# Convolution, routing and expert layers on one core: the first key's weights loaded and split one half batch earlier, the weights' transfers issued one step later and load first

## The chip, the cores and the metric

The kernel runs on one core of one Trainium2 chip. The metric is the device time of one execution in microseconds (us); lower is better. The engines are TensorE (PE, with its weight loads as PEld), VectorE (DVE), ScalarE (ACT), GpSimd (POOL) and SyncE (SP), which here only issues transfers.

## The reference

```python
# B = 8, S = 3584, D = 192; 8 heads of 24 channels, 7 taps
w = softmax(weight)                       # [8, 7]
out = einsum('hk,bskhg->bshg', w, unfold(pad(x)))   # causal convolution, per head
x = out.reshape(28672, 192)
logits = x @ w_gate                       # [28672, 8]
# greedy: all (token, expert) pairs in falling order of the logit; a token takes
# the first expert that has room; each expert takes 28672 / 8 = 3584 tokens
for e in range(8):
    h = maximum(x[mask_e] @ w1[e], 0)     # w1 192 x 1024
    out[mask_e] = h @ w2[e]               # w2 1024 x 192
```

## The kernel before

**Stage 1, convolution.** The tokens go through in 16 half batches of 1792. For each, `load` brings `X` in three transfers, `conv` makes eight PE products `cv` with a Toeplitz matrix (one per head), and ACT copies each into `a`; then ACT's queue issues the store `attn<-a`. The `cv` products take turns on four PSUM banks, so PE can be at most four ahead of ACT's copies. Between the heads, `mid(h)` puts in other work: DVE's transposes `aT<-a`, the gate products `pl` of an earlier half batch, their copy `L` on ACT, a transpose `pt`, and DVE's `M`. Pieces of the routing (who goes to which expert) are run by `bg.hook` as generators; their PE products and copies are named `bg`, `oa`, `X`, `asm`, `ja`. When the first list `ja` is there, GpSimd gathers (`xg`) the tokens of the first two tiles.

**Stage 2, expert layers.** `FFN.run` takes 56 tiles of 512 tokens. In a step `i` it runs, for `f` from 0 to 7: the first-layer product `ph` of tile `i` (`l1`, five matmuls), ACT's `hh` and DVE's `hl` from it, a part of the preparation of tile `i+1` (PE's `px`, then `xa` and `xd` on ACT and DVE), half of a second-layer product `y` of tile `i-1` (`l2`), and one call of `wsplit`. Matrices are kept as a high and a low float32r part, so that few passes give float32 accuracy.

**The weights.** A key is an expert at one of its visits. On the first visit, `wload` brings a part of the raw weights into a tile `raw` (pool `wr`, four buffers): `a` and `d` are halves of the first matrix (`d` in two transfers), `w` a quarter of the second. The pieces of a key come in the order a, d, a, d, w, w, w, w. `wsplit` takes the next piece, if its step has come: ACT copies the high part (`w<-raw`), an engine given by the caller subtracts for the low part (`w<-raw,w` or `dl<-raw,w`), SP stores both parts in DRAM (`kw`, `kd`, `kv`) for the second visit, and then the load of the piece four ahead is issued (lines 1200 to 1246). All these transfers stand in SP's one queue, in the order of the code, and each waits there for what it needs. Transfers also take eight completion semaphores in turn, and one waits for the transfer eight before it.

For the first key the four loads are issued at the start of half batch 13 (line 1554) and the first four pieces are split in half batches 14 and 15, at every other head, with GpSimd as the subtracting engine (line 1568). Its second matrix and all other keys are split by DVE in the steps of stage 2. Key 0's second matrix and key 1's first are split in step 0. After step 0, `tail` makes the gate products of half batches 14 and 15 on PE, each with `L`, a transpose and `M` behind it; then step 1 starts.

Of the kernel before, what the change touches and what calls it, by code (L numbers as in the profile page):

```python
# [6 lines left out]
F32 = mybir.dt.float32  # L7
# [21 lines left out]
class Meter:  # L29


    def __init__(self, pace, name, eng):
        self.pace, self.name, self.eng = pace, name, eng
# [1099 lines left out]
class FFN:  # L1133
# [3 lines left out]
    def __init__(self, tc, nc, attn, w1, w2, out, ident, wr, drm):  # L1137
        self.tc, self.nc = tc, nc

        self.kept1 = [drm.tile([128, 3, F], F32, name="kw%d" % e) for e in range(NE)]  # L1140
        self.keptd = [drm.tile([64, F], F32, name="kd%d" % e) for e in range(NE)]
        self.kept2 = [drm.tile([128, 8, 2 * D], F32, name="kv%d" % e) for e in range(NE)]
        self.attn, self.w1, self.w2, self.out, self.ident, self.wr = attn, w1, w2, out, ident, wr
        self.bg = lambda: None
        self.busy = lambda: False
        self.WT, self.RAW, self.XG, self.XT, self.H, self.Y, self.XS = {}, {}, {}, {}, {}, {}, {}
        self.wpa, self.wpb, self.DL = [None, None], [None, None], [None, None]
        self.scat, self.late = [], []
        self.free = set()
        self.xg = None  # L1150

# [47 lines left out]

    def wsplit(self, i, eng):  # L1200

        if self.done == len(self.pieces) or self.pieces[self.done][0] > i:
            return
        V, A = self.nc.vector, self.nc.scalar
        _, ky, j, what, q = self.pieces[self.done]
        wp = self.wpa[j]
        e = ky[0]
        if what == "W1" or (what, q) == ("a", 0):
            W = wp.tile([128, 3, F], FR, name="w1")
            self.WT[ky] = [W[:, 0], W[:, 1], W[:, 2], self.DL[j]]  # L1210
        if what == "W1":
            self.nc.sync.dma_start(W.bitcast(F32), self.kept1[e])
            self.nc.sync.dma_start(self.DL[j][0:64].bitcast(F32), self.keptd[e])
            self.done += 1
            return
        if what == "W2":
            t = self.wpb[j].tile([128, 8, 2 * D], FR, name="w2")
            self.WT[ky].append(t)
            self.nc.sync.dma_start(t.bitcast(F32), self.kept2[e])
            self.done += 1  # L1220
            return
        r = self.RAW.pop(self.done)
        if (what, q) == ("w", 0):
            self.WT[ky].append(self.wpb[j].tile([128, 8, 2 * D], FR, name="w2"))
        t = self.WT[ky]
        if what == "w":
            r = r[:, 0:2 * D].rearrange("p (k d) -> p k d", d=D)
            s = slice(2 * q, 2 * q + 2)
            hi, lo = t[4][:, s, 0:D], t[4][:, s, D:2 * D]
        else:  # L1230
            s = slice(512 * q, 512 * q + 512)
            hi, lo = (t[0][:, s], t[1][:, s]) if what == "a" else (t[2][:, s], t[3][0:64, s])
        A.activation(hi, r, AF.Copy)
        n = 64 if what == "d" else 128
        eng.tensor_tensor(lo, r[0:n], hi[0:n].bitcast(F32), op=OP.subtract)
        S = self.nc.sync
        if what == "w":
            S.dma_start(self.kept2[e][:, s], t[4][:, s].bitcast(F32))
        elif what == "a":
            S.dma_start(self.kept1[e][:, 0, s], hi.bitcast(F32))  # L1240
            S.dma_start(self.kept1[e][:, 1, s], lo.bitcast(F32))
        else:
            S.dma_start(self.kept1[e][:, 2, s], hi.bitcast(F32))
            S.dma_start(self.keptd[e][:, s], lo.bitcast(F32))
        self.done += 1
        self.wload()


    def gather(self, i, idx, rows=NTOK, clear=None):
# [162 lines left out]
def moe_kernel(ctx, tc, x, weight, wg, w1, w2, out):  # L1412
    nc = Pace(tc.nc)
    V, P = nc.vector, nc.gpsimd
# [4 lines left out]
    with ExitStack() as cw:  # L1419
# [11 lines left out]
        ff = FFN(tc, nc, attn, w1, w2, out, r.ident, wr, drm)  # L1431
# [99 lines left out]
        def hook(at):  # L1531
            nc.pe = max(nc.pe, PERIOD * at / 8 + START)
            bg.hook(1.5)
            if not got and len(bg.gens) == 4:
                first()
                got.append(at)
            elif got and at >= got[0] + 10 and at % 8 in (2, 5) and todo:
                for _ in range(2):
                    todo.pop(0)()
# [6 lines left out]
        for i in range(NHB):  # L1546
            if i + 3 < NHB:
                k.load(i + 3)
            if i == 4:
                r.consts_late()  # L1550
            if i == 13:
                cx[0].close()
                for _ in range(4):
                    ff.wload()
                ff.wpool(cw, 0, **late)

            def mid(h):

                if i and h == 0:
                    for u in range(4):  # L1560
                        left.append(partial(k.transp, i - 1, u))
                        if i > 1:
                            left.append(partial(gate, i - 2, u) if u < 3 else partial(end, i - 2))
                for _ in range(2 if got else 1):
                    if left and (i < LAG or got):
                        left.pop(0)()
                if i >= 14 and h % 2:
                    ff.wsplit(-1, P)
                hook(8 * i + h)

            k.conv(i, mid)
# [82 lines left out]
```

## Time and profile before

| | |
|---|---|
| three timed runs, us | median 1287.89, 1285.86 to 1289.23 |
| the profiled execution, us | 1280.46 |
| its span, first to last instruction, us | 1278.6 |
| mean granted clock of TensorE | 0.988 of 2.4 GHz |
| busy, us: PE, PEld | 1228.0 (96%), 1052.9 (82%) |
| busy, us: DVE, ACT, POOL | 993.4 (78%), 551.0 (43%), 510.0 (40%) |
| moved by DMA | 193.02 MB, 151 GB/s |

All rows are of the profiled execution. A time in a row counts from the start of the span. In a row of the windows, the first number after the stretch is its length; a busy time stands with the number of instructions in brackets. In a row of the timeline, `[1.80 <-ACT w L55]` means that the engine stood idle for 1.80 us before the instruction and that ACT's instruction on `w` ended that wait; `x4` means four such instructions, with their common length. A convolution product and a gate product are float32 and count as two matmuls each. SPq and ACTq are the issues of transfers. A line number of 55 is that of a helper that records every operation, so the names tell what an instruction is.

### The profile page before, as it was taken

The page shows a single profiled execution, that of the slowest core. Times are in us where ns is not written, and L with a number is a line of the kernel's source. Part 1 is how long each engine was busy: PE and PEld are TensorE (multiplying, and loading weights), DVE is VectorE, ACT ScalarE, POOL GpSimd, SP SyncE. Part 2 cuts the span into 40 slices and gives each one's busy share as a digit, 9 for nine tenths or more (in the row PEclk, how much of TensorE's full clock was granted, in tenths as well). Part 3 has the DMA queues.
Part 4 walks back from the last instruction along what each step waited for, and adds up shares of the span by engine and source line. Part 5 has one row for each costly group of instructions (what it writes and reads, how often), then busy time and mean ns, then how long its engine had stood idle before and what let it go on. Part 6 is the DMA issues. An engine that isn't in the chain of part 4 may idle for free.

```text
span 1278.6 us, 21798 instructions
## 1 busy us (share of the span) xinstructions
PE 1228.0 (96%) x7847; PEld 1052.9 (82%) x7847; DVE 993.4 (78%) x2229; ACT 551.0 (43%) x1220; POOL 510.0 (40%) x504
## 2 busy tenths in 40 slices
PE   5989979999999999999799999999999999999997
PEld 2445558889889888898689999999999999999997
DVE  7398569799989998998666777777777777777772
ACT  4544545856344434443243333333333333333332
POOL 3000335364354454343234444444444444444422
PEclk9999989999999999999899999999999999999999
DMA  9999797899533343433543423232413232231100
GB/s 239 345 332 301 249 330 262 277 316 320 187 105 133 102 151 95 148 131 104 126 131 101 165 76 102 96 117 74 151 47 113 77 102 97 68 120 47 47 25 29
DMA packets 100579, 193.02 MB, mean 151 GB/s; under 512 B 19232, under 2 KB 64752, under 8 KB 96240
## 3 DMA queue, kind: packets, MB, share of 16 engines
q1 hardware_dynamic: 57856, 115.15, 27.7%
q0 software_dynamic: 21504, 44.07, 11.6%
q10 hardware_dynamic: 21104, 32.34, 7.7%
q8 instruction: 63, 1.03, 0.3%
q14 instruction: 52, 0.43, 0.1%
HBM read 116.02 MB, written 75.50 MB: 150 GB/s over the span
## 4 chain that ended last, share of the span: by engine, by line
PE 85%; DMA 6%; DVE 5%; ACT 2%; issue 1%; POOL 1%; SPq 1%; POOLq 0%; ACTq 0%; DVEq 0%
PE ph L55 39%; PE y L55 38%; PE cv L55 3%; DMA X<-in_x_dram 3%; PE bg L55 3%; DMA raw<-in_moe_w_dram 2%; PE px L55 1%; DVE X L55 1%; PE pl L55 1%; DVE aT L55 1%; DVE hl L55 1%; ACT a_d L55 1%; POOL xg L1254 0%; DMA X<-otab 0%; ACT w L55 0%
## 5 line engine op out<-in xcount | busy, mean ns | idle before, releaser
L55 PE MATMUL y<-w,hh 128*128 128x384 f32 x1792 | 540.9, 357 | 0.0
L55 ACT ACTIVATE hh<-ph 128x512 fp32r<-128x512 f32 x448 | 268.1, 598 | 498.8 <-PE ph L55 497.6
L55 PE MATMUL y<-w,hl 128*128 128x192 f32 x1792 | 449.4, 251 | 0.0
L55 DVE SCALAR_TENSOR_TENSOR hl<-ph,hh 128x512 fp32r<-128x512 f32 x448 | 308.1, 688 | 146.2 <-ACT hh L55 142.2
L55 PE MATMUL ph<-xa,w 128*128 128x512 f32 x1344 | 396.4, 403 | 4.0 <-DVE hl L55 4.0
L55 PEld LDWEIGHTS y<-w,hl 128*128 128x128 f32 x1792 | 341.6, 191 | 15.1
L55 PEld LDWEIGHTS y<-w,hh 128*128 128x128 f32 x1792 | 337.0, 188 | 19.0 <-issue 2.2
L1329 POOL DMA_INDIRECT out_dram<-yo,ib x128 | 127.9, 999 | 288.4 <-DVE yo L55 278.6
L55 PEld LDWEIGHTS ph<-xa,w 128*128 128x128 f32 x1344 | 219.3, 190 | 24.8 <-DVE hl L55 5.6
L1329 POOL DMA_INDIRECT out_dram<-yo,ia x96 | 111.8, 1164 | 255.2 <-DVE yo L55 224.0
L55 DVE STREAM_TRANSPOSE xs<-xg 32x256 f32<-32x256 f32 x480 | 177.0, 369 | 8.2
L55 PE MATMUL ph<-xd,w 128*128 128x512 f32 x448 | 177.7, 397 | 1.7 <-DVE xd L55 1.7
L55 PE MATMUL ph<-xd,dl 128*128 128x512 f32 x448 | 174.9, 390 | 0.4 <-DVE dl L55 0.4
L1254 POOL DMA_INDIRECT xg<-attn,jb x128 | 138.2, 1080 | 57.1 <-issue 40.6
L1254 POOL DMA_INDIRECT xg<-attn,ja x96 | 110.3, 1149 | 32.1 <-issue 25.8
L55 PE MATMUL cv<-X,TH 118*128 118x384 f32 x256 | 102.8, 528 | 17.5 <-DVE TH L55 12.6
L55 ACT ACTIVATE yt<-y 128x192 f32<-128x192 f32 x224 | 73.6, 329 | 103.8 <-PE y L55 102.0
L55 DVE TENSOR_TENSOR yo<-y,yt 128x192 f32<-128x192 f32 x224 | 79.5, 355 | 40.3 <-ACT yt L55 37.6
L55 PEld LDWEIGHTS ph<-xd,w 128*128 128x128 f32 x448 | 84.3, 188 | 21.6 <-DVE xd L55 2.1
L55 PEld LDWEIGHTS ph<-xd,dl 128*128 128x128 f32 x448 | 84.5, 189 | 20.4 <-DVE dl L55 0.7
L55 PEld LDWEIGHTS cv<-X,TH 118*128 118x128 f32 x256 | 45.3, 197 | 51.5 <-issue 14.1
L55 ACT ACTIVATE a<-cv 128x384 f32<-128x384 f32 x128 | 59.6, 492 | 55.4 <-PE cv L55 37.7
(237 smaller groups left out, 901.3 us busy)
## 6 DMA issues: line engine op xcount, KB each, us to landing
w<-kw SPq DMA_DIRECT2D x16, 1536.0 KB, 8.0
w<-kv SPq DMA_DIRECT2D x16, 1536.0 KB, 7.1
attn<-a ACTq DMA_DIRECT2D x16, 1344.0 KB, 11.8
kw<-w SPq DMA_DIRECT2D x48, 256.0 KB, 4.3
kv<-w SPq DMA_DIRECT2D x32, 384.0 KB, 4.1
X<-in_x_dram SPq DMA_DIRECT2D x17, 672.0 KB, 14.5
X<-in_x_dram ACTq DMA_DIRECT2D x15, 672.0 KB, 10.9
raw<-in_moe_w_dram SPq DMA_DIRECT2D x32, 192.0 KB, 3.9
```

Source lines behind the costliest of these rows:

```text
L55: return f(*a, **k)
L1254: self.nc.gpsimd.indirect_dma_start(out=t[:, b], out_offset=None, in_=self.attn[0:rows], in_offset=bass.IndirectOffsetOnAxis(ap=idx[b], ax ...
L1329: st = self.nc.gpsimd.indirect_dma_start(out=self.out, out_offset=bass.IndirectOffsetOnAxis(ap=idx, axis=0), in_=o, in_offset=None, bounds ...
```

## The change

The four loads of the first key move from the start of half batch 13 to that of 12. The calls of `wsplit` in stage 1 begin in half batch 13 instead of 14, with DVE as the subtracting engine. And the transfers that belong to a piece (the load of a piece four ahead, and the stores) are kept as a function `moves`, which the next call of `wsplit` runs first; in it the load comes ahead of the stores.

```diff
     def wsplit(self, i, eng):
 
+        if self.moves:
+            self.moves()
+            self.moves = None
         if self.done == len(self.pieces) or self.pieces[self.done][0] > i:
             return
...
         S = self.nc.sync
-        if what == "w":
-            S.dma_start(self.kept2[e][:, s], t[4][:, s].bitcast(F32))
-        elif what == "a":
-            S.dma_start(self.kept1[e][:, 0, s], hi.bitcast(F32))
-            S.dma_start(self.kept1[e][:, 1, s], lo.bitcast(F32))
-        else:
-            S.dma_start(self.kept1[e][:, 2, s], hi.bitcast(F32))
-            S.dma_start(self.keptd[e][:, s], lo.bitcast(F32))
+
+        def moves():
+
+            self.wload()
+            if what == "w":
+                S.dma_start(self.kept2[e][:, s], t[4][:, s].bitcast(F32))
+            elif what == "a":
...
+        self.moves = moves
         self.done += 1
-        self.wload()
...
+            if i == 12:
+                for _ in range(4):
+                    ff.wload()
             if i == 13:
                 cx[0].close()
-                for _ in range(4):
-                    ff.wload()
                 ff.wpool(cw, 0, **late)
...
-                if i >= 14 and h % 2:
-                    ff.wsplit(-1, P)
+                if i >= 13 and h % 2:
+                    ff.wsplit(-1, V)
```

On ACT, this is the order around half batch 13 (`a<-cv` are the copies of the convolution, `w` the high parts of key 0, `X` and `asm` belong to the routing):

```order
 L204 DMA attn<-a 112x4x768
 L55 ACTIVATE a<-cv 128x16x24
+L55 ACTIVATE w_1442<-raw 128x512
 L55 ACTIVATE X_1119<-bg 128x512
 L55 ACTIVATE a<-cv 128x16x24 x2
-L55 ACTIVATE X_1465<-bg 128x1024 x2
+L55 ACTIVATE w_1442<-raw 128x512
+L55 ACTIVATE X_1474<-bg 128x1024 x2
+L55 ACTIVATE a<-cv 128x16x24 x2
+L55 ACTIVATE w_1442<-raw 128x512
+L55 ACTIVATE a<-cv 128x16x24
+L55 ACTIVATE asm<-bg 128x192
```

Three of the four copies now stand ahead of `asm`, and the fourth follows behind one more `a`; before, all four stood behind the next `attn`, in half batches 14 and 15.

On SP, this is the stretch of before behind the first loads of key 0 (`raw` of 128x2x192 is a quarter of the second matrix, `raw` of 128x512 or 64x512 belongs to the first matrix of key 1; `kw_83`, `kd_91` and `kv_99` are the stores of key 0):

```order
L1240 DMA kw_83<-w_1548 128x512
L1241 DMA kw_83<-w_1548 128x512
L1195 DMA raw<-in_moe_w_dram 128x2x192
L1243 DMA kw_83<-w_1548 128x512
L1244 DMA kd_91<-dl 64x512
L1195 DMA raw<-in_moe_w_dram 128x2x192
```

And this is the same stretch of the change:

```order
L1195 DMA raw<-in_moe_w_dram 128x2x192
L1247 DMA kw_83<-w_1442 128x512
L1248 DMA kw_83<-w_1442 128x512
L1195 DMA raw<-in_moe_w_dram 128x2x192
L1250 DMA kw_83<-w_1442 128x512
L1251 DMA kd_91<-dl 64x512
```

Each load now stands ahead of the two stores that it stood behind.

Later in SP's queue, around the fourth key (`kw_86`, `kd_94`), the routing writes a table and reads it back (`otab`, `X`). Before:

```order
L1240 DMA kw_86<-w_2650 128x512
L1241 DMA kw_86<-w_2650 128x512
L1195 DMA raw<-in_moe_w_dram 128x2x192
L542 DMA otab_82<-X_2311 128x2048
L559 DMA X_2711<-otab_81 16x16x128 x4
L559 DMA X_2711<-otab_82 16x16x128 x4
L1243 DMA kw_86<-w_2650 128x512
```

And with the change:

```order
L559 DMA X_2707<-otab_81 16x16x128 x4
L559 DMA X_2707<-otab_82 16x16x128 x4
L1195 DMA raw<-in_moe_w_dram 128x2x192
L1247 DMA kw_86<-w_2650 128x512
L1248 DMA kw_86<-w_2650 128x512
```

The first second-matrix load of that key moves from ahead of the table's transfers to behind them. Elsewhere PE, DVE and ACT keep their order in stage 2.

## Rows read from the trace of the kernel before

**Rows 1.** Windows: busy us of PE, PEld, DVE, ACT, POOL; clock; DMA share; GB/s:

```profile
160.00:180.00 20.00, 14.56 (x75) 9.93 (x77) 13.34 (x21) 9.69 (x20) 10.91 (x11) 0.89 0.95 303
...
180.00:200.00 20.00, 18.03 (x189) 15.18 (x182) 14.77 (x36) 9.27 (x23) 1.25 (x1) 0.94 0.88 308
...
280.00:300.00 20.00, 20.00 (x119) 18.13 (x118) 18.91 (x41) 14.79 (x40) 14.08 (x10) 1.00 0.97 324
```

**Rows 2.** Chain of waits, 159 to 183 us (start, length, what):

```profile
159.54 2.23 DMA kd<-dl
...
161.84 0.31 ACTq L204
...
165.86 8.89 DMA raw<-in_moe_w_dram
...
176.85 5.33 DMA raw<-in_moe_w_dram
...
182.20 0.63 ACT w L55
```

**Rows 3.** Timeline, ACT and DVE, 159 to 176 us (start, length, idle before):

```profile
159.98 1.29 ACT L55 ACTIVATE a<-cv 128x384 f32<-128x384 f32 x3
...
171.65 0.53 ACT L55 ACTIVATE w<-raw 128x384 fp32r<-128x384 f32 x1 [3.49 <-DMA raw<-in_moe_w_dram]
...
172.21 0.56 DVE L55 TENSOR_TENSOR w<-raw,w 128x384 fp32r<-128x384 f32 x1 [1.80 <-ACT w L55]
...
174.78 0.52 ACT L55 ACTIVATE w<-raw 128x384 fp32r<-128x384 f32 x1 [2.12 <-DMA raw<-in_moe_w_dram]
...
175.33 0.56 DVE L55 TENSOR_TENSOR w<-raw,w 128x384 fp32r<-128x384 f32 x1 [1.95 <-ACT w L55]
```

**Rows 4.** Timeline, SP's issues of the weights' transfers, 132 to 177 us:

```profile
132.01 0.47 SPq L1193 DMA_DIRECT2D raw<-in_moe_w_dram  x1
...
175.92 0.32 SPq L1238 DMA_DIRECT2D kv<-w  x1
...
176.28 0.52 SPq L1192 DMA_DIRECT2D raw<-in_moe_w_dram  x1
```

**Rows 5.** Instructions on the tile raw (ns min/median/max, first and last start):

```profile
L55 ACT ACTIVATE w<-raw x64: 508/578/641, 144.1 to 322.7; 128x512 fp32r<-128x512 f32 x32, 128x384 fp32r<-128x384 f32 x32
...
L55 DVE TENSOR_TENSOR w<-raw,w x46: 536/550/694, 167.6 to 324.7; 128x384 fp32r<-128x384 f32 x32, 128x512 fp32r<-128x512 f32 x14
...
L1235 POOL TENSOR_TENSOR w<-raw,w x2: 1280/1284/1288, 144.8 to 159.5; 128x512 fp32r<-128x512 f32 x2
...
DMA to landing us min/median/max: 2.8/4.3/9.5
```

**Rows 6.** Timeline, half batch 13: ACT, PE and DVE, 139 to 145 us:

```profile
139.03 1.94 ACT L55 ACTIVATE X<-bg 128x1024 bf16<-128x1024 bf16 x2 [0.53 <-PE bg L55]
...
141.80 2.83 PE L55 MATMUL cv<-X,TH 118*128 118x384 f32 x8
...
142.37 0.18 DVE L55 TENSOR_SCALAR m_f<-asm 128x32 f32<-128x32 f32 x1 [6.78 <-ACT asm L55]
```

**Rows 7.** Timeline, PE, the gate products of half batches 14 and 15:

```profile
179.00 2.79 PE L55 MATMUL bg<-aT,c_mu 128*32 128x128 f32 x48
...
183.46 1.52 PE L55 MATMUL bg<-aT,c_mu 128*32 128x128 f32 x48
```

**Rows 8.** Windows of 2 us around two falls of the granted clock:

```profile
174.00:176.00 2.00, 0.87 (x4) 0.37 (x2) 0.67 (x2) 1.01 (x2) 1.70 (x2) 0.87 1.09 315
...
182.00:184.00 2.00, 0.80 (x21) 0.68 (x25) 1.02 (x3) 1.23 (x4) 0.00 (x0) 0.92 1.04 353
...
622.00:624.00 2.00, 0.00 (x0) 0.00 (x0) 1.83 (x7) 0.00 (x0) 0.00 (x0) 0.66 1.15 95
```

**Rows 9.** Timeline, SP and ACT, 228 to 239 us, weights of the fourth key:

```profile
228.52 5.02 SPq L559 DMA_DIRECT2D X<-otab  x8
...
238.16 0.51 ACT L55 ACTIVATE w<-raw 128x384 fp32r<-128x384 f32 x1
```

More of the change, by code (lines that the diff above doesn't have):

```diff
@@ L1147, in __init__ @@
         self.wpa, self.wpb, self.DL = [None, None], [None, None], [None, None]
-        self.scat, self.late = [], []
+        self.scat, self.late, self.moves = [], [], None
         self.free = set()
@@ L1236, in wsplit @@
         S = self.nc.sync
-        if what == "w":
-            S.dma_start(self.kept2[e][:, s], t[4][:, s].bitcast(F32))
-        elif what == "a":
-            S.dma_start(self.kept1[e][:, 0, s], hi.bitcast(F32))
-            S.dma_start(self.kept1[e][:, 1, s], lo.bitcast(F32))
-        else:
-            S.dma_start(self.kept1[e][:, 2, s], hi.bitcast(F32))
-            S.dma_start(self.keptd[e][:, s], lo.bitcast(F32))
+        def moves():
[3 more added lines that the diff above has]
+            elif what == "a":
+                S.dma_start(self.kept1[e][:, 0, s], hi.bitcast(F32))
+                S.dma_start(self.kept1[e][:, 1, s], lo.bitcast(F32))
+            else:
+                S.dma_start(self.kept1[e][:, 2, s], hi.bitcast(F32))
+                S.dma_start(self.keptd[e][:, s], lo.bitcast(F32))
+        self.moves = moves
         self.done += 1
-        self.wload()
     def gather(self, i, idx, rows=NTOK, clear=None):
```

## The prediction

> **What bounds the kernel now.** The profiled execution has a span of 1278.6 us and a time of 1280.46 us; the median of the three timed runs, 1287.89 us, is 0.6% above it. All terms below are worked out on the span and taken off the median at the end. About 0.3% (3.9 us) is what a measurement of this kernel can tell from no change.
>
> I read the windows first. From 280 us on TensorE (PE) is busy for the whole of a window at full clock, so that what the weights' transfers and splits cost there is hidden. In the two windows after the product stage starts, 160 to 200 us, PE is busy for 14.56 and 18.03 us of 20, and the clock is 0.89 and 0.94 [rows 1]. These holes add up to 5.44 + 1.97 = 7.4 us. They are all that this edit can take away, beside what the low clock costs.
>
> Next the chain of waits says what fills the holes. It runs from a store of key 0's split weights (`kd<-dl`) through a copy issue on ScalarE's queue, then a load of raw weights of 8.89 us, then another of 5.33 us, to ScalarE's `w` copy at 182.20 [rows 2]. The timeline shows the same from the engines' side: ScalarE stands still 3.49 us and 2.12 us for two parts of key 0's second matrix, and VectorE (DVE), which subtracts behind it, 1.80 us and 1.95 us [rows 3]. So the stage starts too early for its weights. On SP, the second-matrix loads stand behind stores that wait for GpSimd's subtractions, which in turn stand behind eight gathers on GpSimd. One part took 9.5 us to land, where the median is 4.3 [rows 5].
>
> **The change, part by part.**
>
> *Loads in half batch 12.* SP's order has nothing between the old and the new place, so the six transfers leave at the same times; 0. The last of them left at 132.01 [rows 4].
>
> *Four subtractions from GpSimd to DVE, one half batch earlier.* GpSimd loses four of 1.28 us. DVE gains four of 0.55 to 0.69 us [rows 5], some 2.5 us, three of them into a wait of 6.78 us [rows 6]; the fourth comes behind the list and moves the transposes by under 1 us. 0, and 2.5 us at most if that cover were gone.
>
> *Four copies on ScalarE, from half batches 14 and 15 into 13.* Each is about 0.58 us [rows 5], 2.3 us together, in an engine with little room: one gap there is 0.53 us [rows 6]. What is queued behind them are the evacuations of the convolution, for which PE waits through four PSUM banks. PE runs four heads in a row there, 2.83 us [rows 6], or 0.7 us a head, so four banks let ScalarE fall about 2 us behind. I take 0; the bounds are 0 and 2.3 us.
>
> *Second-matrix loads of key 0.* The four parts now leave as soon as the first four are split, in half batches 13 and 14, and are in place before 160 us. Three things follow.
>
> 1. ScalarE's `attn` store at 161.84 started 0.07 us after the `kd` store landed (159.54 + 2.23), though the last copy before it ended at 159.98 + 1.29 = 161.27 [rows 2, 3]. The `kd` store is now over by then: 0.55 us earlier for `xd`, and for all behind it.
> 2. DVE's waits of 1.80 and 1.95 us vanish [rows 3]: 3.75 us. What is late next is the second half of key 1's last first-matrix part. It may leave when key 0's last part is split. ScalarE copies it, in order, ahead of the logits `L` on which PE waits.
> 3. That load used to stand behind a `kv` store, 0.36 us on SP (175.92 to 176.28) [rows 4]; now the load is first. It took 5.33 us [rows 2]. Five stores and three loads of key 0, by their shapes 1.6 MB, now lie before 160 us instead of after it, so I take 4.8 us, between 5.33 and the median 4.3 [rows 5]: 0.5 us less. The bounds are the same rows' 2.8 us and 9.5 us.
>
> `L` and all behind it come 0.55 + 3.75 + 0.36 + 0.5 = 5.2 us earlier.
>
> [...]
>
> *The clock in the hole that is left.* Without the waits tile 0's last product ends 4.3 us sooner, and another 1.3 us if it runs at full clock (the gate products behind it show the ratio, 2.79 us slow and 1.52 us full [rows 7]): near 173.4 instead of 179.00. Half batch 14's gate products end at about 175, and `L` can't start before 182.83 − 5.2 = 177.6. So a hole of some 2.6 us stays, just ahead of half batch 15's gate products. Before, the clock fell from 2.4 to 1.2 GHz in the window of 174 to 176 us, when PE was busy 0.87 us of 2, and came back in that of 182 to 184; at 622 to 624 it fell with PE wholly idle [rows 8]. Before, that cost nothing on the chain: the slow gate products, 2.79 us, ended at 181.8, ahead of the late copy at 182.20 [rows 7, 2]. If it falls now, it falls on work that all the rest waits for: 2.79 − 1.52 = 1.27 us on the second gate products [rows 7], and about 0.9 us on the products behind them until it returns; 2.2 us, with bounds of 0 and 4 us (a slow stretch of 8 us full of work). I take 2.2.
>
> [...]
>
> *Loads first, one step late, for all keys.* An SP issue waits for the same subtraction as before, whatever its place in the program; only neighbours in SP's order matter. The one bad place is key 3: its first second-matrix load now stands behind eight `X<-otab` loads, until 228.52 + 5.02 = 233.54 us, and is wanted at 238.16 [rows 9]. With the median landing of 4.3 us [rows 5] it is there at 237.9, with 6 us 1.4 us late. I take 0, at most 1.4. The gain of loads first elsewhere is hidden under a full PE [rows 1]: 0.
>
> **Sum.** −5.2 + 2.2 = −3.0 us: a span of 1275.6, and 1287.89 − 3.0 = 1284.9 us.
>
> **The rivals.**
>
> - *The clock falls* (forecast): 1284.9, 0.50. Its own range is 1283 to 1287.
> - *The clock holds.* For it: a mean of 0.89 over 160 to 180 [rows 1] says that the clock was full until about 175.6, through most of the 5.44 us of holes, and a landing of 4.3 us makes the new hole 0.5 us shorter. 1287.89 − 5.2 = 1282.7, 0.32.
> - *The gain is given back.* The DMA engines are busy 0.88 to 0.97 of the time until 300 us [rows 1]. If they set the pace, raw parts land later by what PE gained, and holes open between 200 and 300 us. Against it: PE is full at 280 to 300 us with 0.97. About 0.5 us would stay: 1287.4, 0.09.
> - *Slower.* ScalarE meets the part whose load left at 132.01 [rows 4] about 1.2 us behind `asm`, which DVE had at 142.37 [rows 6]: near 143.6 us. It decides from a landing of 11.6 us on: ScalarE stops, the evacuations behind it stop, and about 1 us later PE does, which opens a hole there and lets the clock fall. A landing 3 us past that point costs 2 us of wait and 4 us of slow clock: 3.0 less than the forecast turns into 1287.89 − 3.0 + 6 = 1290.9. Against it is the longest landing of rows 5, 9.5 us. 0.09.
>
> **How the numbers follow.** Faster by over 0.3% (under 1284.0) are most of the clock that holds (0.30 of 0.32) and a quarter of the clock that falls (0.13). Slower by over 0.3% is the last rival (0.08) and little else (0.02). That is 0.43 faster, 0.47 same, 0.10 slower. The range goes from 2 us under the clock that holds (a landing of 2.8 us instead of 4.8 [rows 5]) to the case given back and 0.9 us above it, since the runs of before lie up to 1.3 us above their median: 1280.7 to 1288.3. The slower rival is left out.
>
> **What would show it.** Right: no ScalarE wait on `raw` between 160 and 172 us; GpSimd without subtractions; ScalarE's last `w` copy of key 1's first matrix at about 177 instead of 182.20 [rows 2]; the second gate products from about 178 instead of 183.46 [rows 7]; PE over 16.5 us busy in 160 to 180. The clock of the windows 176 to 184 tells the first two cases apart. Wrong: a new PE wait on ScalarE's `a` in 138 to 146 us, the `w` copies of half batch 13 waiting for `raw`, or holes of PE between 200 and 300 us that weren't there.

## The result and the profile after

| | before | after |
|---|---|---|
| median, us (22 runs each, beside one another) | 1287.89 | 1293.07 |
| lowest and highest, us | 1285.07, 1295.80 | 1290.05, 1295.16 |
| the profiled execution, its span, us | 1280.46, 1278.6 | 1292.08, 1290.3 |

The ratio, run against run, is 1.0033, with an interval of 1.0023 to 1.0043: slower, by 4.2 us (5.2 between the medians), where 3.0 us less were forecast. One thing has to be known for all that follows: the kernel before itself took 1288, 1289 and 1285 us on three occasions (an occasion is one set of runs on one chip) and 1280, 1279 and 1280 us on three others, so each ratio is taken against runs of the kernel before beside it, and rows are compared within like occasions where there is a profile for it. The occasions of 1289 and 1285 were on one chip, the three quick ones on three other chips, and for the first one the chip isn't on record; so what belongs to an occasion and what to a chip can't be told apart here. By its time, the trace of before that the prediction read (1280.46) is of the quick kind, the trace of after of the long kind.

The windows of the changed kernel, in the columns of [rows 1]:

```profile
140.00:160.00 20.00, 16.20 (x156) 7.62 (x155) 12.62 (x27) 7.89 (x21) 9.02 (x9) 0.91 0.83 275
160.00:180.00 20.00, 16.77 (x127) 11.56 (x126) 16.00 (x25) 11.97 (x25) 9.32 (x9) 1.00 0.69 219
180.00:200.00 20.00, 15.60 (x136) 13.04 (x137) 10.32 (x29) 6.32 (x17) 1.24 (x1) 0.83 0.81 278
```

The trace of before has this for the first of them:

```profile
140.00:160.00 20.00, 20.00 (x206) 10.63 (x205) 13.64 (x31) 13.40 (x36) 12.74 (x13) 1.00 0.72 237
```

PE lost 3.8 us between 140 and 160 us, where the trace of before has it busy throughout, gained 2.2 us in the next window and lost 2.4 us in the third. The chain of waits, against [rows 2]:

```profile
149.88 4.96 another core or an unknown queue
...
174.78 7.99 DMA raw<-in_moe_w_dram
182.85 0.63 ACT w L55
```

The two loads of 8.89 and 5.33 us have become one of 7.99 us, and a new link stands ahead. The timeline of ScalarE and PE shows both, against [rows 3] and [rows 7]:

```profile
148.50 0.31 ACTq L204 DMA_DIRECT2D attn<-a  x1
149.39 0.49 ACT L55 ACTIVATE a<-cv 128x384 f32<-128x384 f32 x1 [0.93 <-DVE aT L55]
154.82 0.22 ACT L55 ACTIVATE L<-pl 128x64 f32<-128x64 f32 x1 [4.93 <-remote]
155.30 0.48 PE L55 MATMUL pt<-ident,L 128*128 128x128 f32 x1 [3.11 <-ACT L L55]
165.52 0.50 PE L55 MATMUL ph<-xd,w 128*128 128x512 f32 x1 [1.16 <-DVE xd L55]
...
166.84 0.51 ACT L55 ACTIVATE w<-raw 128x384 fp32r<-128x384 f32 x1
...
171.65 0.52 ACT L55 ACTIVATE w<-raw 128x384 fp32r<-128x384 f32 x1
...
182.85 0.63 ACT L55 ACTIVATE w<-raw 128x512 fp32r<-128x512 f32 x1 [4.01 <-DMA raw<-in_moe_w_dram]
183.85 0.47 PE L55 MATMUL bg<-ident,L 128*128 128x128 f32 x1 [4.41 <-ACT L L55]
184.25 2.79 PE L55 MATMUL bg<-aT,c_mu 128*32 128x128 f32 x48
187.59 0.48 PE L55 MATMUL bg<-ident,L 128*128 128x128 f32 x1 [0.55 <-ACT L L55]
```

ScalarE stands still for 4.93 us ahead of a copy `L`, between the `attn` of half batches 14 and 15 (below: **the stop**). The `pl` products that `L` reads ended at 151.34, and the view names as releaser neither an engine nor a queue of the program ("remote"). The semaphores in the same trace do name one: `L` waits for the semaphore that PE raises when products are done, and that one rises at 154.80, 0.02 us ahead of `L` (more under **Open**). PE waits 3.11 us for that copy. In step 0 the four `w` copies of key 0's second matrix wait for nothing now, but the last part of key 1's first matrix, 4.01 us, so `L` of the tail still comes late. The windows of 2 us, against [rows 8]:

```profile
156.00:158.00 2.00, 2.00 (x18) 0.60 (x17) 1.88 (x3) 0.96 (x3) 0.00 (x0) 0.50 0.26 94
158.00:160.00 2.00, 2.00 (x23) 1.14 (x20) 1.10 (x2) 0.49 (x1) 0.00 (x0) 0.83 0.02 8
...
184.00:186.00 2.00, 2.00 (x37) 1.65 (x41) 0.59 (x2) 0.28 (x1) 0.00 (x0) 0.50 1.00 343
186.00:188.00 2.00, 1.45 (x22) 0.97 (x15) 0.00 (x0) 0.43 (x2) 0.00 (x0) 0.50 0.32 122
```

The granted clock falls to 0.50 behind both holes, and PE is busy in the slow stretches: both falls are paid. In the first of them two matmuls of the convolution start 0.64 us apart (155.57 and 156.21); at 1.00 it is 0.32 us.

What SP issues in half batches 13 and 14 now:

```profile
135.59 1.50 SPq L1247 DMA_DIRECT2D kw<-w  x1
...
142.94 2.05 SPq L1250 DMA_DIRECT2D kw<-w  x1
145.04 2.45 SPq L1251 DMA_DIRECT2D kd<-dl  x1
```

From the first to the last these are eight stores, six `kw` of 256 KB and two `kd` of 128 KB: 1.84 MB. In the trace of before, three of them left in half batch 14 and five at the start of step 0:

```profile
144.73 0.33 SPq L1240 DMA_DIRECT2D kw<-w  x1
...
148.84 0.87 SPq L1243 DMA_DIRECT2D kw<-w  x1
159.54 0.47 SPq L1244 DMA_DIRECT2D kd<-dl  x1
...
163.14 2.67 SPq L1244 DMA_DIRECT2D kd<-dl  x1
```

From 135 to 156 us the DMA share is now 1.01, where the trace of before has 0.75, and the gathers and `attn` move in the same stretch.

### The profile page after: what moved, and what is told of

Same layout as the page of the kernel before. It is cut to its first block, busy times and chain, and to the rows that moved or that the text cites. A ratio compares the mean times of both kernels' runs of the same rounds, so it can differ in the third digit from the quotient of the medians.

```text
span 1290.3 us, 21779 instructions
## 1 busy us (share of the span) xinstructions
PE 1230.4 (95%) x7847; PEld 1054.5 (82%) x7847; DVE 995.6 (77%) x2233; ACT 549.6 (43%) x1220; POOL 506.0 (39%) x500
## 3 DMA queue, kind: packets, MB, share of 16 engines
q8 instruction: 63, 1.03, 0.3%
## 4 chain that ended last, share of the span: by engine, by line
PE 85%; DVE 6%; DMA 4%; ACT 2%; issue 1%; SPq 1%; POOL 0%; another core or an unknown queue 0%; ACTq 0%; POOLq 0%; DVEq 0%
PE ph L55 38%; PE y L55 37%; PE cv L55 4%; PE bg L55 3%; PE px L55 1%; DMA X<-in_x_dram 1%; DVE aT L55 1%; DVE X L55 1%; DMA raw<-in_moe_w_dram 1%; PE pl L55 1%; DMA wgr<-in_moe_w_gate_dram 1%; DVE hl L55 1%; DVE oa L55 1%; DMA kv<-w 0%
```

## The experiments

Two theories were set against each other. *Bunching*: key 0's transfers, moved into the end of the convolution, crowd the DMA engines there and stop ScalarE. *Order*: loads first and one step late push back loads that are waited for, for all keys.

Three intervals from the timelines tell most: from the `attn` issue of half batch 12 to that of 15 (the end of the convolution), from the first `ph<-xd,w` to the first `bg<-ident,L` (step 0; the forecast takes 3.75 + 0.36 + 0.5 = 4.6 us off it), and from there to the second one (the gate products of half batch 15: 2.3 us at full clock, 3.7 at half). "Before" is the median of the kernel before on the same occasion.

| run | before | ratio, interval | attn 12 to 15 | step 0 | gate |
|---|---|---|---|---|---|
| before, as first profiled | 1280 | | 26.24 | 19.64 | 2.33 |
| r_before | 1280 | 1.0000, 0.999 to 1.001 | 26.25 | 19.47 | 3.18 |
| before_c | 1285 | one run | 26.82 | 19.93 | 3.74 |
| after | 1288 | 1.0033, 1.0023 to 1.0043 | 31.46 | 18.33 | 3.74 |
| after_b | 1289 | 1.0022, 1.0003 to 1.0042 | 31.43 | 18.11 | 3.74 |
| r_after | 1280 | one run | 25.68 | 18.37 | 3.74 |
| after_c | 1279 | 0.9988, 0.9974 to 1.0002 | 25.67 | 17.33 | 3.64 |
| after_d | 1280 | 0.9988, 0.9971 to 1.0005 | 27.25 | 17.58 | 3.75 |
| early | 1280 | 0.9983, 0.9972 to 0.9995 | 25.69 | 17.28 | 3.74 |
| early_b | 1289 | 1.0017, 0.9998 to 1.0036 | 32.45 | 18.71 | 3.71 |
| early_first | 1289 | 1.0016, 0.9997 to 1.0036 | 32.94 | 17.54 | 3.74 |
| moves | 1280 | 1.0000, 0.9986 to 1.0015 | 27.14 | 18.46 | 3.74 |
| early_late_v | 1279 | 1.0000, 0.9989 to 1.0012 | 26.81 | 18.35 | 3.75 |
| hold | 1289 | 0.9981, 0.9963 to 1.0000 | 31.63 | 14.63 | 2.32 |
| hold_b | 1285 | 0.9958, 0.9941 to 0.9975 | 32.33 | 14.51 | 2.33 |
| before_hold | 1285 | 0.9962, 0.9942 to 0.9982 | 27.31 | 15.98 | 2.33 |
| hold_all | 1285 | 1.0041, 1.0022 to 1.0060 | 26.86 | 14.57 | 2.32 |
| hold_two | 1279 | 0.9946, 0.9926 to 0.9966 | 25.69 | 13.69 | 2.33 |
| hold_two_b | 1280 | 0.9936, 0.9913 to 0.9959 | 25.69 | 13.59 | 2.33 |
| double | 1280 | 1.0050, 1.0034 to 1.0066 | 32.70 | 17.59 | 3.65 |

**Both kernels again.**

> The kernel before, unchanged, profiled and timed against itself. The profile of before that the prediction read took 1280.46 us, under the lowest timed run; the profile of after took 1292.08 us. If that trace was an unusually quick execution, this one has a span near 1286 us and shows part of the late holes of after (330, 380 and 540 us), whatever the change did. If the trace was ordinary, the span is near 1279 us and the late holes are absent. The ratio should be 1.000 within 0.002.

> The changed kernel again, for a second profile. Holes that the change causes must be at the same places again: ScalarE idle for about 4.9 us ahead of a copy L between half batches 14 and 15 (near 154 us), the wait of 4 us for the last part of key 1's first matrix (near 183 us), and the wait for key 2's weights near 250 us. A hole that is not there again belongs to the one execution.

The trace of before was ordinary for its occasion: the second span is 1277.3 us. The second profile of after has the hole of step 0 again (5.96 us ahead of `L`) but not the stop. So the stop belongs to the occasion as well as to the kernel, and the next runs had to tell whether to the kernel at all.

**The two halves of the change.** `early` moves the loads and the splits and leaves the transfers in their old order; `moves` does the opposite.

```diff
+            if i == 12:
+                for _ in range(4):
+                    ff.wload()
...
-                if i >= 14 and h % 2:
-                    ff.wsplit(-1, P)
+                if i >= 13 and h % 2:
+                    ff.wsplit(-1, V)
```

> Only the first key is early: its loads in half batch 12, its four splits with VectorE from half batch 13 on; all transfers stay in the old order and place. Theory bunching (key 0's transfers, moved into the end of the convolution, crowd the DMA engines there): this alone loses what the change lost, +4 to +6 us, with ScalarE's hole near 154 us. Theory order (load first and one step late is what hurts, for all keys): this alone gains 2 to 5 us, as the prediction's steps 1 and 2 said, and the wait at 183 us is short.

> Only the order of the transfers is changed, for all keys: one step late, load first; stage 1 as before, with the splits by GpSimd from half batch 14 on. Theory bunching: no difference, 0 to 1 us. Theory order: +4 to +6 us, with the waits for raw near 183 and 250 us as after, and no hole of ScalarE at 154 us.

On an occasion of 1280 us the new order does nothing, and the early splits gain 2.2 us by the ratio (2.8 between the medians). The theory that the order hurts is out there; the bunching theory is not confirmed either, since nothing was lost.

> The changed kernel timed against the one before, together with the three kernels below. The loads early alone gave 0.9983 and the new order of the transfers alone 1.000. If both add up, this gives 0.998. If the new order takes the gain of the early loads away once both are there (the last half of key 1's first matrix lands in 6.9 us instead of 4.7), it gives 1.000. If the first result, 1.0033, is the change's own and not that of one occasion, it gives 1.003, and the wait of 4.9 us near 154 us is there again.

> The loads and splits of the first key early, all transfers in the old order, as before. Every theory: 0.998 again; this is the base for the next two.

The next occasion was a long one, and `early`, the same file, turned from 0.9983 to 1.0017. In its timeline the stop is back, and again the view names no releaser:

```profile
149.06 0.31 ACTq L204 DMA_DIRECT2D attn<-a  x1
155.42 0.22 ACT L55 ACTIVATE L<-pl 128x64 f32<-128x64 f32 x1 [4.98 <-remote]
```

The changed kernel and `early` are alike (1.0022 and 1.0017): the loss lies in the early half of the change, not in the order.

**Load first, without the step of delay** (`early` with the load ahead of its piece's stores):

```diff
         S = self.nc.sync
+        self.wload()
         if what == "w":
...
         self.done += 1
-        self.wload()
```

> As the kernel above, and each load stands ahead of the stores of the piece that freed its buffer, not a step later. The prediction's step 3 (a load first leaves 0.36 us sooner and lands no later): 0.3 to 0.9 us under the kernel above. If the transfers only trade places on full DMA engines: the same as above within 0.5 us. If the load first is what hurts in the change: +2 us or more over the kernel above. If the step of delay is what hurts: this one is like the kernel above, and the change as a whole 2 us or more slower than both.

1.0016 against 1.0017: step 3 of the prediction gained nothing that can be measured. `L` of step 0 came 1.2 us sooner in this profile. At the start of step 2, 0.8 us of that is left, and a longer wait of PE for the routing at 227 us (1.42 us against 0.75 in `early_b`) takes it back.

**Stores held back.** From the fifth piece on, the stores wait in a list and are issued four pieces later, load first:

```diff
+        due = self.done < len(self.pieces) and self.pieces[self.done][0] <= i
+        if self.moves and (len(self.moves) > 3 or not due):
+            self.moves.pop(0)()
+        if not due:
+            return
...
+        self.moves.append(moves)
+        if self.done < 4:
+            self.moves.pop()()
```

> Loads early and first, and from the fifth piece on the stores of a piece are issued four pieces later, so that the loads of key 1's first matrix have no store of key 0's second matrix (4 x 384 KB) beside them. If the DMA engines set the pace in step 0 (the prediction's third case): ScalarE's waits for raw between 160 and 178 us fall from about 5 us to under 2 us, the hole of TensorE ahead of the first L of the tail from 4.9 to under 3 us, 2 to 3 us under the two kernels above. If each load's own latency sets the pace: no change.

It beat `early_first` by 0.35%. In `hold_b`, the same kernel on the next occasion, PE's wait ahead of the tail is this:

```profile
180.30 0.33 PE L55 MATMUL bg<-ident,L 128*128 128x128 f32 x1 [0.52 <-ACT L L55]
182.63 0.33 PE L55 MATMUL bg<-ident,L 128*128 128x128 f32 x1 [0.55 <-ACT L L55]
```

The wait of 4.41 us is down to 0.52, step 0 (14.63 us in `hold`, 14.51 here) is 2.6 us or more shorter than in the kernels that split early and store beside its loads, and the clock does not fall (the gate products take 2.32 and 2.33 us). With the stores of key 0's second matrix held, 2.9 us of step 0 are gone (14.63 us, 17.54 in `early_first`).

**What the long occasion does to the kernel before, and the first four stores.**

> The kernel before, for a profile beside those of the next three. In all four kernels with the loads early, timed where the kernel before took 1289 us, ScalarE stood still for about 4.95 us ahead of one copy L (two stops of 2.76 and 3.31 us with the stores held), and TensorE's clock fell behind it. If the early transfers cause that, it is absent here even at a time of 1289 us; if it comes with the occasion, it is here too. The extra time of 23.5 instead of 22 us near 275 us, and of 188 to 190 instead of 184 us between 520 and 710 us, should be here in an execution of 1289 us, since the kernels differ nowhere there.

> Loads early and first, stores four pieces later from the fifth piece on, as run before (0.9981): the base of the next two. 0.997 to 0.999 where the kernel before takes 1289 us; where it takes 1280 us and early loads gain 2.8 us, 5 us or more below it, 0.995.

> The first key loaded and split where it was before (half batches 13 to 15, GpSimd), only loads first and stores four pieces later from the fifth piece on. If the stores beside the loads were all of what step 0 waits for, this alone gains 2 to 4 us over the kernel before, and the early loads add nothing to it. If the start of the second matrix's loads counts, as the prediction's step 1 and 2 said, ScalarE still waits for two of its parts between 165 and 175 us (5.6 us in the kernel before), and the gain is under 1 us.

> All stores of split weights are held twelve pieces back, also those of the first four pieces, so that from 130 to 180 us only loads, the stores attn and the gathers move. Theory bunching: ScalarE's stops ahead of the copies near 154 us go (5 to 6 us of its idle time, some 3 us of TensorE's), and the clock does not fall there: 2 to 5 us under the kernel above wherever that one has these stops, and no change where it does not. If the stops come from the early loads or from neither: no change, 0 within 0.5 us, or slower if the held stores collide with the transfers of steps 1 to 3.

`before_c` has no stop at 1285 us. Its rows at the place of the stop:

```profile
151.03 0.31 ACTq L204 DMA_DIRECT2D attn<-a  x1
151.67 0.22 ACT L55 ACTIVATE L<-pl 128x64 f32<-128x64 f32 x1 [0.67 <-PE pl L55]
...
157.66 0.23 ACT L55 ACTIVATE L<-pl 128x64 f32<-128x64 f32 x1 [1.90 <-PE cv L55]
```

`hold_b` has it beside it, `before_hold` and `hold_all` have not. These are the rows of `hold_b` and then of `hold_all`:

```profile
154.09 0.22 ACT L55 ACTIVATE L<-pl 128x64 f32<-128x64 f32 x1 [4.89 <-remote]
153.88 0.22 ACT L55 ACTIVATE L<-pl 128x64 f32<-128x64 f32 x1 [2.56 <-PE cv L55]
```

`hold_b` and `hold_all` differ before 160 us only in the eight stores of the first four pieces. So on this occasion the stop went with those stores, as far as one profile of each can show it. `before_hold` gains as much as `hold_b`: with the stores of step 0 out of the way, the early splits add nothing where they bring the stop. `hold_all` was the slowest of its occasion all the same, and not where I had looked. ScalarE's `w` copies wait later for stores that have become too late:

```profile
258.48 0.53 ACT L55 ACTIVATE w<-raw 128x384 fp32r<-128x384 f32 x1 [5.17 <-DMA kv<-w]
269.60 0.63 ACT L55 ACTIVATE w<-raw 128x512 fp32r<-128x512 f32 x1 [5.61 <-DMA kw<-w]
```

The copy writes a tile whose last contents are still being stored, and these waits repeat until 325 us.

**Held long once, then short.** Nothing is stored before the thirteenth piece; from there on two pieces a call until four are left waiting (against `hold`):

```diff
-        if self.moves and (len(self.moves) > 3 or not due):
-            self.moves.pop(0)()
+        for _ in range(2):
+            if self.done > 11 and self.moves and (len(self.moves) > 3 or not due):
+                self.moves.pop(0)()
...
-        if self.done < 4:
-            self.moves.pop()()
```

> Loads and splits early; the stores of the first twelve pieces are held back until the thirteenth is split, then two pieces are stored in a call until four are left waiting, and from there on four are held as in the two kernels that gained 0.4%. Theory bunching (the stores of the first four pieces between 135 and 156 us stop ScalarE): no stop ahead of the copy L near 154 us, TensorE busy over 7 of 8 us between 148 and 156 us (4.9 with the stop), attn to attn around it 10 to 11.5 us instead of 15.3 to 16.8, and no collisions later, so 0.992 to 0.995. If the held stores just collide in step 1: 0.996 or more, with holes between 190 and 240 us.

> The kernel with the stores of the first twelve pieces held back (0.9946 where the kernel before took 1279 us). Theory bunching, on an occasion with the stop: no stop here, and a ratio of 0.990 to 0.995, further from the changed kernel than there. On one without: 0.9946 again, within 0.002.

0.9946 and 0.9936, the best of all, and faster than both kernels. Windows of `hold_two`:

```profile
140.00:160.00 20.00, 18.85 (x190) 9.71 (x188) 15.43 (x35) 11.08 (x30) 10.18 (x11) 1.00 0.67 213
160.00:180.00 20.00, 17.31 (x170) 13.44 (x171) 17.45 (x29) 11.96 (x27) 8.74 (x8) 1.00 0.77 239
180.00:200.00 20.00, 20.00 (x136) 17.91 (x134) 18.08 (x44) 10.70 (x23) 5.46 (x5) 1.00 0.92 322
```

The clock stays full, and the DMA share from 140 to 180 us is 0.67 and 0.77, where the changed kernel on the same occasion (`after_c`) has 0.92 and 0.90. Both occasions were quick ones, on which the changed kernel has no stop either; whether it keeps the stop away on a long one was not seen.

**The changed kernel with late splits, and with its first stores doubled.** `early_late_v` sets `i >= 13` back to 14; `double` issues the stores of the first four pieces twice.

> The changed kernel a third time. If the kernel before takes 1285 us or more: the stop of ScalarE near 154 us and a ratio of 1.001 to 1.004. If it takes 1280 us: no stop, ratio 0.998 to 1.001.

> The changed kernel with one line undone: the loads of the first key stay in half batch 12, but its four splits run in half batches 14 and 15 as before (VectorE still subtracts), so that its stores and the second-matrix loads leave as late as before. Theory bunching by the stores: no stop near 154 us, since no store is there; attn to attn 9.5 to 10.5 us; ratio near that of the new order alone, 1.000, under the changed kernel's by 0.001 to 0.003 where that one has the stop. If the early raw loads or VectorE's subtractions cause the loss: the stop, or the changed kernel's ratio, is here too.

> The changed kernel a fourth time, beside the next two. Its ratio so far: 1.0033 and 1.0022 where the kernel before took 1288 and 1289 us and ScalarE stopped near 154 us; 0.9988 where it took 1279 us and did not stop. Again the one pair or the other, and nothing between.

> The changed kernel with the stores of the first four pieces issued twice (0.9 MB more between 135 and 160 us, some 3 us at the 310 GB/s that the DMA engines move there). Theory bunching: the stop of ScalarE near 154 us is there even where the changed kernel has none, or 2 to 4 us longer where it has one; +2 to +6 us over the changed kernel. If the stop has nothing to do with these stores: the same as the changed kernel within 1 us.

The changed kernel came out at 0.9988 twice and showed no stop. `early_late_v` gave 1.0000: on this occasion, early loads and VectorE's subtractions by themselves do nothing. Since the occasion had no stop, it could not tell the loads from the stores there. `double` took 7.3 us more than the changed kernel beside it (1286.40 − 1279.15; the stores that it adds are 1.84 MB, twice what the expectation says), and ScalarE stopped:

```profile
159.54 0.31 ACTq L204 DMA_DIRECT2D attn<-a  x1
159.97 0.49 ACT L55 ACTIVATE a<-cv 128x384 f32<-128x384 f32 x1 [8.16 <-DMA raw<-in_moe_w_dram]
160.84 0.47 PE L55 MATMUL pt<-ident,L 128*128 128x128 f32 x1 [5.31 <-ACT L L55]
```

But this is another stop: its chain names a store, the load issued behind it, and then ScalarE's own issue:

```profile
146.90 7.44 DMA kw<-w
...
155.72 3.74 DMA raw<-in_moe_w_dram
...
159.54 0.31 ACTq L204
```

This `attn` left 0.08 us behind the load's landing (155.72 + 3.74) and 7.7 us behind the end of ScalarE's last copy (151.81); in the trace of after it left 0.04 us behind that copy (148.46, 148.50). So `double` shows that stores there can stop ScalarE and what it costs; it does not show how the changed kernel's own stop comes about.

## Why the prediction was wrong

**Right, at their size.** The loads in half batch 12, the subtractions on DVE and ScalarE's four copies cost nothing that shows: in two of three profiles on quick occasions the end of the convolution is no longer than before (25.7 against 26.2 us). The copies ran at 133.21 to 139.81 without a wait for `raw`, and `m_f`, which [rows 6] has at 142.37, started at 139.63. `xd` came sooner as said: PE's wait for it is 1.16 us against 1.69 in the trace of before. The waits of [rows 3] for key 0's second matrix are gone. Loads first and late for all keys are worth nothing (`moves` 1.0000), and the fourth key's `w` copy at 240.94 waits for nothing, its load having left at 236.34.

**The first step that failed: point 3 of the second-matrix loads, "I take 4.8 us, between 5.33 and the median 4.3".** What is late next was named correctly, the last part of key 1's first matrix. But its load took 7.99 us in the trace of after, 7.77 in `after_b`, 8.15, 7.09 and 7.31 in `r_after`, `after_c` and `after_d`; 5.33, 5.99 and 6.66 in three profiles of before. I took the transfers that moved ahead of 160 us as relief. But most of what was gained by starting sooner was spent again on the load: in the trace of after it left 9.3 us after step 0 began, in that of before 13.3 us, so 4.0 us sooner, and it took 2.7 us longer. In the same few microseconds four parts of 384 KB are stored, the first at 170.57 and the last at 175.88 in the trace of after. Step 0 became 1.7 us shorter (the mean of the five profiles of after, 17.94, against 19.68 for the three of before), not 4.6. `hold` shows that these stores are what the load is slow beside: 3 us more come off step 0 once they are held, and in `hold_two` 6.0 us in all (13.64 against 19.68). This is the rival in which the gain is given back and the DMA engines set the pace; I had put it between 200 and 300 us and gave it 0.09. Nor is the load really first: only the last of the four stores has moved behind it, and three still leave ahead of it (170.57, 172.38 and 173.47, the load at 174.78). A load issued first shows no gain in the time in `early_first` either, 1.0016 against 1.0017.

**The clock** was sized rightly and booked wrongly. The gate products behind the hole cost 3.74 instead of 2.33 us, 1.41 for a forecast 1.27. But two of three profiles of before pay part or all of it too (3.18 and 3.74), so only some 0.6 us of it are new (3.72 against 3.08, means of five and three). The traces give the clock as a share, 1.00 or 0.50; at 1.00 the matmul behind a product `bg<-F,U` of 512 columns starts 0.216 us after it in the trace of before, 2.4 columns a nanosecond, and this is all that the runs show of the prediction's 2.4 GHz.

**The step that failed most is one that the sum did not have: eight stores, 1.84 MB, which now all leave in half batches 13 and 14.** Before, three of them left in half batch 14 and the rest from 159.54 us on. I took five stores off step 0 as relief, costed the load issues, the copies and the subtractions in half batches 13 and 14, and the stores there not at all. On the occasions of 1280 us they are free: attn 12 to 15 is 25.7 us, 0.5 less than before, in two of three profiles (27.25 in the third, where PE waited for a gather). With −1.7 in step 0 and +0.6 for the gate that makes −1.6 us; measured: 1279.15 − 1279.74 and 1278.34 − 1279.33, and 0.9988 of 1279.5 is −1.5. On the long occasions the stop is there, in six of six profiles of kernels with all eight stores there (4.9 us, or two stops of 2.76 and 3.31), and in none of the three with at most three of them there (`before_c`, `before_hold`, `hold_all`). The same interval is then 31.4 instead of 26.4 (mean of the three profiles of before): +5.0. With −1.7 and +0.6 the sum is +3.9 us; measured +4.2 (1.0033) and +2.8 (1.0022). Against `before_c` alone, the one profile of the kernel before from a long occasion, the three terms are +4.6, −1.7 and 0, together +2.9 us. So on the long occasions the forecast of 3.0 us faster missed the sign by the stop. On the quick ones step 0 gained 2.9 us less than forecast, of which the smaller price of the clock (0.6 us instead of 2.2) gave 1.6 back. That these stores bring the stop is shown by which kernels have it, not by how it comes about.

The slower rival had the mechanism's second half, ScalarE stops, PE stops, the clock falls, and a price of +3.0, but tied it to a late `raw` in half batch 13; that did not happen. And the base was read past a warning: the trace was 0.6% under the timed median, so by its time it was of an occasion on which this kernel behaves otherwise.

**Open.** What holds ScalarE in the stop is PE's signal; what holds the signal is open. The products that raise the semaphore for which `L` waits ended at 151.35 and 152.19 us in the trace of after. Their two rises, which should lie 0.8 us apart, are on record at 154.80 and 154.84, 2.6 us behind the last product, and `L` starts between them. The other stops are alike (2.6 to 2.7 us; in `hold` 1.8 and 1.9). Such late rises of PE's semaphore mark the long occasions as a whole: in each of their nine profiles, the kernel before included (`before_c`), 14 to 47 rises come more than 0.5 us behind the product that should have raised them; in the eleven profiles of quick occasions, the trace of before included, none comes more than 0.1 us behind. The rises of ScalarE and VectorE are on time in all twenty, within 0.03 us. (Left out are the last microseconds of each span, from 1250 us on. The ends of products are modelled by the profile.)

The same nine profiles also lack records: 6 to 8% of PE's rises, 10 to 12% of ScalarE's and 11 to 14% of VectorE's are missing, where the eleven others lack at most one of each. So a rival that no run tests is that writing the profile's own records holds PE back on these occasions, and that the long time and the stop come from there. The change's stores would then only decide where it bites.

In the trace of after the DMA share is 0.94 in the window of 154 to 156 us, where the stop ends, and 0.26 in the next, so it ends about when the queues run empty; and on quick occasions a share of 0.98 to 1.03 in the same stretch brings no stop (`after_c`, `after_d`). Queues 8 and 14, whose packets the profile marks as instructions, aren't what is late: none of these packets lies in five of the six stops, and in `hold` one ends 0.3 us after the stop began. Nor is it known how much of the extra time between 300 and 700 us on the occasion of 1289 is the kernel's own, since no profile of before was taken there; the ratios hold it either way.

## What to carry to other kernels

When an edit moves a transfer, give a price to everything that rides with it, the stores above all, and ask of the place it goes to what else is moving there: a wait that ends on a DMA can be slow in landing rather than late in starting, and starting sooner then buys little (here a load left 4.0 us sooner and took 2.7 us longer). A store whose data is needed again only much later is the first thing to move out of a stretch in which loads are waited for (2.9 us of step 0 between `early_first` and `hold`); but held too long it keeps its tile from being written again (waits of 5.17 and 5.61 us in `hold_all`), so hold stores back for a stage and then catch up, not for good. Compare the profiled execution with the median first, and where they differ by more than the effect to be measured, take a second profile before summing anything. And where a view names no releaser, look up the semaphore itself in the trace before thinking of a transfer.

## What the runs showed of the hardware

- With the DMA engines full (share 0.97 to 1.02 from 148 to 156 us in the six profiles), ScalarE stood still for 4.9 us because the semaphore of PE that it waited for rose 2.6 us after PE's last product had ended by the profile (in `hold`, 1.8 and 1.9 us). The same kernel did so on two occasions (`after`, `after_b`) and not on three others (`r_after`, `after_c`, `after_d`) with a share of 0.98 to 1.03.
- The time of one kernel differed by 0.8% between occasions on different chips (1279.3 to 1289.0 us), over twice the effect under study, and the effect changed its sign between them.
- A load took longer to land with stores beside it, in these runs. A load of 128 KB with four stores of 384 KB around it took 5.3 to 6.7 us in the three traces of before and 6.1 and 7.7 in `early` and `early_b` (stores first), 7.1 to 8.2 us in the five of the changed kernel (load ahead of the last store), and 3.66 us with the stores held back (`hold_two`):

```profile
168.95 3.66 DMA raw<-in_moe_w_dram
```
